# Attention over 32 heads beside a Mish layer: head quads outside, row- and column-tiled matmuls, exponentials shared by three engines, an order from a virtual clock

## The chip, the cores and the metric

The kernel runs on one core of one Trainium2 chip. A core has five engines with a queue of instructions each: TensorE (PE; the profile lists its weight loads apart, as PEld), VectorE (DVE), ScalarE (ACT), GpSimd (POOL) and SyncE (SP, which here issues DMAs). Each queue runs in its written order; the engines wait for each other through semaphores. Matmuls write to PSUM, eight banks of 512 fp32 columns on 128 partitions. The metric is the device time of one execution in microseconds; the number compared is the median of several runs. Beside it stands one profiled execution with a row for each instruction.

## The reference

x is 2048 rows (tokens) of 640, in bf16. The result is a gated mix of attention and a dense layer, both of x:

```python
g = _sigmoid((x * gate_w).sum(-1, keepdims=True))
# A: q, k, v = x @ wqkv, 32 heads of 20
scores = jnp.einsum("bhqd,bhkd->bhqk", q, k) * 20 ** -0.5
p = _softmax(scores, axis=-1)
o = jnp.einsum("bhqk,bhkd->bhqd", p, v)
a = o.reshape(B, S, D) @ wo
# B: x (640) -> 1536 -> 640
h = jnp.einsum("bsd,df->bsf", x, w1) + b1
act = h * jnp.tanh(softplus(h))          # Mish
b = jnp.einsum("bsf,fd->bsd", act, w2)
return g * a + (1 - g) * b
```

32 heads times 2048 x 2048 scores are 134 million exponentials: 1,024 tiles of 128 x 1024.

## The kernel before, in words

Queries are cut in four chunks of 512 (`qc`, the outer loop), keys in 16 tiles of 128 (`j`), heads in 16 groups of two (`g`, the middle loop). Weights for four heads are copied into zeroed tiles so that each head's 20 rows start at a multiple of 32 partitions. `emit_group` runs one group over the 16 key tiles. At each it writes the transposed scores of two heads, keys on partitions and 512 queries in columns, into one PSUM tile `Sp` of 1,024 columns (L395), two matmuls of 20 rows on different 32-row strips of the array (`tile_position`); exponentiates it in one ScalarE instruction into `E` (L406); and multiplies by V with `E` as the weights: eight loads of 128 x 128 and eight matmuls that stream 21 columns, 20 of V and a column of ones for the softmax's sum (L412), which add up in `acc`. After 16 key tiles VectorE divides by the sums (L421, L423). `Sp` and `E` have two buffers each.

The rest is cut into units in a list with a cost each: projections of k (L143), v (L186) and q (L208); the dense layer's h = x w1 with Mish from an exponential and five VectorE instructions (L223 to L243); w2 (L261); transposes of the output (L288); wo and the mix (L304 to L329). `pump_slot` is called once for each key tile: it adds `slot_credit` (460 in the first chunk, then 340) and runs units from the list while the credit pays their cost. So the order of TensorE's queue is: scores, the eight PV matmuls, perhaps a unit, the next scores. All of x comes in by one transposing DMA at the start (L88), and again for each chunk (L439).

Of the kernel before, what the change touches and what calls it, by code (L numbers as in the profile page):

```python
# [8 lines left out]
P = 128  # L10
# [3 lines left out]
BF16 = mybir.dt.bfloat16  # L14


@with_exitstack
def kernel(
# [13 lines left out]

    _, S, D = A_x.shape
    F = B_w1.shape[1]
    H = 32
    DH = D // H
    KT = D // P
    FT = F // P
    NS = S // P
    QC = 512  # L40
    NQC = S // QC
    NU = QC // P
    NPAIR = H // 4
    NG = H // 2
    ROWB = 32
    inv_sqrt_dh = float(DH) ** -0.5
    CB = 512
    CH = CB // 2

    x2d = A_x[0]  # L50
    out2d = out[0]

    consts = ctx.enter_context(tc.tile_pool(name="consts", bufs=1))
    wqp = consts.tile([P, KT, NPAIR, P], BF16, tag="wqp")
    ident = consts.tile([P, P], BF16, tag="ident")
    wo_sb = consts.tile([P, KT, D], BF16, tag="wo_sb")
    w1_sb = consts.tile([P, KT, F], BF16, tag="w1_sb")
    w2_sb = consts.tile([P, FT, D], BF16, tag="w2_sb")
    b1bf = consts.tile([P, FT], BF16, tag="b1bf")
    b1f = consts.tile([P, FT], F32, tag="b1f")  # L60
    g_t = consts.tile([P, NS], F32, tag="g_t")
    kT_all = consts.tile([P, NPAIR, S], BF16, tag="kT_all")
    VA = consts.tile([P, NS, H, DH + 1], BF16, tag="VA")

    aps = ctx.enter_context(tc.tile_pool(name="aps", bufs=2, space=bass.MemoryType.PSUM))
    xtc_pool = ctx.enter_context(tc.tile_pool(name="xtc", bufs=2))
    qtc_pool = ctx.enter_context(tc.tile_pool(name="qtc", bufs=3))
    e_pool = ctx.enter_context(tc.tile_pool(name="e_pool", bufs=2))
    opool = ctx.enter_context(tc.tile_pool(name="opool", bufs=1))
    otpool = ctx.enter_context(tc.tile_pool(name="otpool", bufs=1))  # L70
    actpool = ctx.enter_context(tc.tile_pool(name="actpool", bufs=1))
    mishp = ctx.enter_context(tc.tile_pool(name="mishp", bufs=2))
    bpool = ctx.enter_context(tc.tile_pool(name="bpool", bufs=2))
    smallp = ctx.enter_context(tc.tile_pool(name="smallp", bufs=2))
    dpool = ctx.enter_context(tc.tile_pool(name="dpool", bufs=1))
    outp = ctx.enter_context(tc.tile_pool(name="outp", bufs=2))

    xt_ctx = ExitStack()
    xt_ctx.__enter__()
    xtpool = xt_ctx.enter_context(tc.tile_pool(name="xtpool", bufs=1))  # L80
    xT = xtpool.tile([P, KT, S], BF16, tag="xT")

    stage_ctx = ExitStack()
    stage_ctx.__enter__()
    stpool = stage_ctx.enter_context(tc.tile_pool(name="stpool", bufs=1))
    Wq = stpool.tile([P, KT, D], BF16, tag="Wq")
    nc.scalar.dma_start(Wq, A_wqkv[:, 0:D].rearrange("(kt p) c -> p kt c", p=P))
    nc.sync.dma_start_transpose(  # L88
        out=xT[:, :, :], in_=x2d.rearrange("s (kt p) -> s kt p", p=P)
    )  # L90
    wv0 = xtpool.tile([P, KT, 4 * DH], BF16, tag="wvp", bufs=2)
    nc.scalar.dma_start(
        out=wv0[:, :, :],
        in_=A_wqkv[:, 2 * D : 2 * D + 4 * DH].rearrange("(kt p) c -> p kt c", p=P),
    )
    gw = xtpool.tile([P, KT, 1], BF16, tag="gw")
    nc.scalar.dma_start(gw, gate_w.rearrange("(kt p o) -> p kt o", p=P, o=1))
    wk0 = xtpool.tile([P, KT, P], BF16, tag="wkp", bufs=2)
    nc.gpsimd.memset(wk0, 0.0)
    for r in range(4):  # L100
        col0 = 64 * (r // 2) + ROWB * (r % 2)
        nc.scalar.dma_start(
            out=wk0[:, :, col0 : col0 + DH],
            in_=A_wqkv[:, D + r * DH : D + (r + 1) * DH].rearrange(
                "(kt p) c -> p kt c", p=P
            ),
        )
    nc.sync.dma_start(b1bf, B_b1.rearrange("(ft p) -> p ft", p=P))
    nc.gpsimd.dma_start(wo_sb, A_wo.rearrange("(kt p) c -> p kt c", p=P))
    nc.gpsimd.dma_start(w1_sb, B_w1.rearrange("(kt p) c -> p kt c", p=P))  # L110
    nc.gpsimd.dma_start(w2_sb, B_w2.rearrange("(ft p) c -> p ft c", p=P))

    nc.gpsimd.memset(wqp, 0.0)
    for h in range(H):
        p, r = divmod(h, 4)
        col0 = 64 * (r // 2) + ROWB * (r % 2)
        nc.gpsimd.tensor_copy(
            out=wqp[:, :, p, col0 : col0 + DH],
            in_=Wq[:, :, h * DH : (h + 1) * DH],
        )  # L120
    stage_ctx.__exit__(None, None, None)
    make_identity(nc, ident)
    nc.vector.tensor_copy(b1f, b1bf)
    nc.gpsimd.memset(VA, 1.0)

    def kt_units(p, wk=None):
        if wk is None:
            wk = xtpool.tile([P, KT, P], BF16, tag="wkp", bufs=2)
            nc.gpsimd.memset(wk, 0.0)
            for r in range(4):  # L130
                h = 4 * p + r
                col0 = 64 * (r // 2) + ROWB * (r % 2)
                nc.sync.dma_start(
                    out=wk[:, :, col0 : col0 + DH],
                    in_=A_wqkv[:, D + h * DH : D + (h + 1) * DH].rearrange(
                        "(kt p) c -> p kt c", p=P
                    ),
                )

        def chunk(sc):  # L140
            pk = aps.tile([P, CB], F32, tag="t")
            for kt in range(KT):
                nc.tensor.matmul(  # L143
                    pk[:, 0:QC],
                    lhsT=wk[:, kt, 0:P],
                    rhs=xT[:, kt, sc * QC : (sc + 1) * QC],
                    start=(kt == 0),
                    stop=(kt == KT - 1),
                )
            nc.vector.tensor_copy(  # L150
                out=kT_all[:, p, sc * QC : (sc + 1) * QC], in_=pk[:, 0:QC]
            )

        return [(1200, (lambda sc=sc: chunk(sc))) for sc in range(NQC)]

    def v_units(p, wv=None):
        if wv is None:
            wv = xtpool.tile([P, KT, 4 * DH], BF16, tag="wvp", bufs=2)
            nc.sync.dma_start(
                out=wv[:, :, :],  # L160
                in_=A_wqkv[:, 2 * D + 4 * p * DH : 2 * D + 4 * (p + 1) * DH].rearrange(
                    "(kt p) c -> p kt c", p=P
                ),
            )

        def unit(st):
            pv = aps.tile([P, CB], F32, tag="t")
            for kt in range(KT):
                lhsT = xT[:, kt, st * P : (st + 1) * P]
                if p == 0:  # L170
                    nc.tensor.matmul(  # L171
                        pv[:, 0 : 4 * DH],
                        lhsT=lhsT,
                        rhs=wv[:, kt, :],
                        start=(kt == 0),
                        stop=False,
                    )
                    nc.tensor.matmul(
                        pv[:, 4 * DH : 4 * DH + 1],
                        lhsT=lhsT,  # L180
                        rhs=gw[:, kt, 0:1],
                        start=False,
                        stop=(kt == KT - 1),
                    )
                else:
                    nc.tensor.matmul(  # L186
                        pv[:, 0 : 4 * DH],
                        lhsT=lhsT,
                        rhs=wv[:, kt, :],
                        start=(kt == 0),  # L190
                        stop=(kt == KT - 1),
                    )
            nc.vector.tensor_copy(  # L193
                out=VA[:, st, 4 * p : 4 * p + 4, 0:DH],
                in_=pv[:, 0 : 4 * DH].rearrange("p (h d) -> p h d", d=DH),
            )
            if p == 0:
                nc.scalar.activation(
                    g_t[:, st : st + 1], pv[:, 4 * DH : 4 * DH + 1], ACT.Sigmoid
                )  # L200

        return [(260, (lambda st=st: unit(st))) for st in range(NS)]

    def qt_unit(p, xTc, qTc_p):
        def unit():
            pq = aps.tile([P, CB], F32, tag="t")
            for kt in range(KT):
                nc.tensor.matmul(  # L208
                    pq[:, 0:QC],
                    lhsT=wqp[:, kt, p, 0:P],  # L210
                    rhs=xTc[:, kt, 0:QC],
                    start=(kt == 0),
                    stop=(kt == KT - 1),
                )
# [131 lines left out]
    def drain_qt(key):  # L346
        fn = qt_pending.pop(key, None)
        if fn is not None:
            fn()
# [177 lines left out]
```

## Time and profile before

| | |
|---|---|
| runs | 1363.54, 1373.24, 1375.19 us; median 1373.24 |
| the profiled execution, first to last instruction | 1383.0 us, 28,359 instructions |
| TensorE busy | 1235.3 us (89%), 12,384 matmuls |
| TensorE weight loads | 589.6 us (43%), 12,384 |
| ScalarE busy | 1053.3 us (76%) |
| VectorE busy | 463.9 us (34%) |
| GpSimd busy | 28.6 us (2%) |
| granted TensorE clock, mean | 0.608 |
| first matmul, first exponential, end of the last exponential | 44.4, 64.3, 1367.6 us |

A line of the costliest groups reads: line of the kernel, engine, operation, output<-inputs, shapes, count | busy us, mean ns of one | idle time of the engine just before, and what ended most of it. The busy time of an engine is the time in which at least one of its instructions runs; matmuls overlap, so a busy TensorE need not be streaming at its peak. The clock is the share of full speed that TensorE was granted.

### The profile page before, as it was taken

Reading aid. Unit: us, or ns where it says so; the run is one execution under the profiler, and the core shown is the slowest. Engines: PE = TensorE matmul, PEld = TensorE weight load, DVE = VectorE, ACT = ScalarE, POOL = GpSimd, SP = SyncE. Lnnn points to the kernel's source line nnn. Section 1 sums busy time; section 2 is a strip of 40 time slices with the busy share of each in tenths; the row PEclk is TensorE's granted clock in tenths of the full one; section 3 lists DMA queues with packets and bytes.
Section 4 is the critical chain, followed back from the end, with each engine's and each line's share of the span. In section 5 each row is a group of like instructions: output and inputs, shape, how many; then the busy total and the mean of one; then the engine's idle time right before and its main releaser. Section 6 shows DMA issues by size and latency. Waiting matters only on the chain.

```text
span 1383.0 us, 28359 instructions
## 1 busy us (share of the span) xinstructions
PE 1235.3 (89%) x12384; PEld 589.6 (43%) x12384; DVE 463.9 (34%) x1093; ACT 1053.3 (76%) x1138; POOL 28.6 (2%) x51
## 2 busy tenths in 40 slices
PE   0699999988999988998889998998889988998887
PEld 0354444544444444443434444443434444453333
DVE  0222222377722576410101477410001476510002
ACT  0286666987768877698998777698998787699995
POOL 7000000000000000000000000000000000000000
PEclk9975555975585555795555555695555555695555
DMA  9600000000000000000000000000000000000000
GB/s 185 109 8 7 8 7 7 2 1 1 13 8 11 11 1 1 1 21 1 1 1 11 11 1 1 1 2 1 1 2 6 16 2 1 1 2 1 1 1 20
DMA packets 53086, 16.91 MB, mean 12 GB/s; under 512 B 49408, under 2 KB 52096, under 8 KB 52960
## 3 DMA queue, kind: packets, MB, share of 16 engines
q1 hardware_dynamic: 47456, 9.30, 4.6%
q0 software_dynamic: 912, 4.75, 1.2%
q10 hardware_dynamic: 4592, 1.03, 0.6%
q8 instruction: 97, 1.59, 0.5%
q14 instruction: 29, 0.24, 0.1%
HBM read 7.21 MB, written 2.62 MB: 7 GB/s over the span
## 4 chain that ended last, share of the span: by engine, by line
PE 67%; ACT 25%; issue 3%; DMA 3%; DVE 1%; ACTq 0%
PE Sp L395 26%; ACT E L406 25%; PE acc L412 15%; PE ph L223 8%; PE pk L143 5%; PE pb L261 4%; DMA xT<-in_A_x_dram 3%; PE pq L208 3%; PE pa L304 3%; PE pv L186 3%; PE pt L288 1%; ACTq L406 0%; PE pv L171 0%; ACT e_sb L231 0%; DVE d L311 0%
## 5 line engine op out<-in xcount | busy, mean ns | idle before, releaser
L406 ACT ACTIVATE E<-Sp 128x1024 bf16<-128x1024 f32 x1024 | 1006.0, 1022 | 223.6 <-PE Sp L395 213.0
L395 PE MATMUL Sp<-qTc_p,kT_all 20*128 20x512 bf16 x2048 | 589.2, 559 | 0.0
L412 PEld LDWEIGHTS <-E 128*128 128x128 bf16 x8192 | 335.7, 106 | 471.1 <-ACT E L406 376.9
L412 PE MATMUL acc<-VA,E 128*128 128x21 bf16 x8192 | 398.1, 182 | 95.5 <-ACT E L406 93.5
L241 DVE RECIPROCAL rd<-rd 128x256 f32<-128x256 f32 x96 | 167.4, 1744 | 0.8
L395 PEld LDWEIGHTS <-kT_all 20*128 20x128 bf16 x2048 | 104.3, 98 | 51.5 <-issue 18.2
L223 PE MATMUL ph<-xTc,w_sb 128*128 128x256 bf16 x480 | 119.0, 403 | 0.1
L421 DVE RECIPROCAL rden<-acc 128x8 f32<-128x8 f32 x64 | 12.4, 193 | 297.4 <-PE acc L412 297.4
L223 PEld LDWEIGHTS <-w_sb 128*128 128x128 bf16 x480 | 51.7, 128 | 57.4 <-issue 42.6
L234 DVE SCALAR_TENSOR_TENSOR e_sb<-e_sb 128x256 f32<-128x256 f32 x96 | 40.4, 421 | 100.5 <-ACT e_sb L231 99.6
L215 DVE CAST qTc_p<-pq 128x512 bf16<-128x512 f32 x32 | 22.1, 691 | 148.8 <-PE Sp L395 98.6
L231 ACT ACTIVATE e_sb<-ph,b1f 128x256 f32<-128x256 f32 x96 | 45.4, 473 | 33.8 <-PE ph L223 29.9
L143 PE MATMUL pk<-xT,wk 128*128 128x512 bf16 x140 | 66.0, 548 | 0.0
L208 PE MATMUL pq<-xTc,wqp 128*128 128x512 bf16 x160 | 64.5, 492 | 0.0
L261 PE MATMUL pb<-w_sb,actT 128*128 128x512 bf16 x192 | 58.0, 419 | 0.1
L150 DVE CAST kT_all<-pk 128x512 bf16<-128x512 f32 x32 | 22.1, 691 | 96.3 <-PE pk L143 96.3
L186 PE MATMUL pv<-wv,xT 128*128 128x80 bf16 x560 | 50.7, 237 | 0.0
L193 DVE CAST VA<-pv 128x80 bf16<-128x80 f32 x128 | 30.4, 243 | 57.7 <-PE pv L186 51.5
L143 PE MATMUL pk<-xT,wk_118 128*128 128x512 bf16 x20 | 7.2, 544 | 44.4 <-DMA xT<-in_A_x_dram 44.4
L243 DVE SCALAR_TENSOR_TENSOR actT<-ph,b1f,rd 128x256 bf16<-128x256 f32 x96 | 45.8, 478 | 0.1
L186 PEld LDWEIGHTS <-xT 128*128 128x128 bf16 x560 | 33.4, 117 | 23.2 <-issue 23.0
L261 PEld LDWEIGHTS <-actT 128*128 128x128 bf16 x384 | 28.5, 101 | 33.3 <-issue 24.1
(101 smaller groups left out, 351.9 us busy)
## 6 DMA issues: line engine op xcount, KB each, us to landing
w_sb<-in_B_w_dram POOLq DMA_DIRECT2D x2, 1920.0 KB, 31.1
out_dram<-ot SPq DMA_DIRECT2D x16, 160.0 KB, 1.8
Wq<-in_A_wqkv_dram ACTq DMA_DIRECT2D x1, 800.0 KB, 4.9
wo_sb<-in_A_wo_dram POOLq DMA_DIRECT2D x1, 800.0 KB, 24.5
wv<-in_A_wqkv_dram SPq DMA_DIRECT2D x7, 100.0 KB, 2.3
wk<-in_A_wqkv_dram SPq DMA_DIRECT2D x28, 25.0 KB, 2.6
wv_114<-in_A_wqkv_dram ACTq DMA_DIRECT2D x1, 100.0 KB, 10.7
wk_118<-in_A_wqkv_dram ACTq DMA_DIRECT2D x4, 25.0 KB, 29.7
```

The costliest lines, as they stand in the source:

```text
L143: nc.tensor.matmul(pk[:, 0:QC], lhsT=wk[:, kt, 0:P], rhs=xT[:, kt, sc * QC : (sc + 1) * QC], start=(kt == 0), stop=(kt == KT - 1),)
L186: nc.tensor.matmul(pv[:, 0 : 4 * DH], lhsT=lhsT, rhs=wv[:, kt, :], start=(kt == 0), stop=(kt == KT - 1),)
L208: nc.tensor.matmul(pq[:, 0:QC], lhsT=wqp[:, kt, p, 0:P], rhs=xTc[:, kt, 0:QC], start=(kt == 0), stop=(kt == KT - 1),)
L223: nc.tensor.matmul(ph[:, 0:CH], lhsT=w1_sb[:, kt, ft * P : (ft + 1) * P], rhs=xTc[:, kt, half * CH : (half + 1) * CH], start=(kt == 0), st ...
L231: nc.scalar.activation(e_sb, ph[:, 0:CH], ACT.Exp, bias=b1f[:, ft : ft + 1], scale=1.0)
L241: nc.vector.reciprocal(out=rd, in_=rd)
L243: nc.vector.scalar_tensor_tensor(out=actT[:, ft, half * CH : (half + 1) * CH], in0=ph[:, 0:CH], scalar=b1f[:, ft : ft + 1], in1=rd, op0=AL ...
L261: nc.tensor.matmul(tile_[:, 0 : col1 - col0], lhsT=actT[:, ft, u * P : (u + 1) * P], rhs=w2_sb[:, ft, col0:col1], start=(ft == 0), stop=(f ...
L304: nc.tensor.matmul(pa[:, :], lhsT=oT[:, ct, u * P : (u + 1) * P], rhs=wo_sb[:, ct, 0:CB], start=(ct == 0), stop=(ct == KT - 1),)
L395: nc.tensor.matmul(Sp[:, QC * t : QC * (t + 1)], lhsT=kT_all[base + ROWB * t : base + ROWB * t + DH, p, j * P : (j + 1) * P,], rhs=qTc_p[b ...
L406: nc.scalar.activation(E[:, :], Sp[:, :], ACT.Exp, scale=inv_sqrt_dh)
L412: nc.tensor.matmul(acc[:, u, t, 0 : DH + 1], lhsT=E[:, QC * t + P * u : QC * t + P * (u + 1)], rhs=VA[:, j, h, 0 : DH + 1], start=first, s ...
```

## The change

The kernel is written anew; the launch is the same. What it does:

- **Loops.** The outer loop is now over quads of four heads, the inner one over the four query chunks (`GROUPS`: for the first six quads all chunks of a quad in a row; quads 6 and 7 chunk by chunk). A group is one quad and one chunk: 16 key tiles x 2 head pairs = 32 units of 128 x 1024 scores. There are 32 groups, 1,024 units. The output of quads 0 to 5 is parked in DRAM (`on_d`) and read back for wo, which runs over quads with zero-padded weights (`wop`).
- **Scores** (`emit_score`, `try_score`): two matmuls of 32 rows (20 and zeros) for a unit; two units together, four row strips, if two score slots are free. Three slots of two PSUM banks, two in the opening.
- **PV** (`emit_pv`): E is the moving operand, 512 columns, and V (20 columns and one of ones, 32 wide) the weights, on a 32-column strip for each head. The four heads of a quad add up in one PSUM bank on four partition strips.
- **Exponentials.** 746 units by ScalarE. The other 278 as bit lines: a VectorE multiply and add turns scores into 16-bit integers that, read as bf16, are a piecewise linear curve near the exponential (`psum_chord`); two copies of that, shifted by 35 and 83, are made by GpSimd, or the first by VectorE (`chord`), and PV adds all three. This approximates the exponential; `CH_OFF` sets the level of the lines so that their sum equals the exponential on average. ScalarE's units are exponentials as before.
- **Normalizing** (`acc_out`): a group's sums go by DMA to 128 partitions, are inverted, go through DRAM and back broadcast over partitions, and GpSimd multiplies.
- **The rest.** x is loaded in 16 plain tiles and transposed by TensorE. Mish is one ScalarE function on 128 x 3072, eight calls. The gate is two exponentials and reciprocals. (1-g) b is parked in DRAM (`b_d`).
- **Order.** `Plan` is a virtual clock with an assumed duration for every instruction. `poll_pe`, `poll_act`, `poll_dve`, `poll_gp` and `poll_sp` choose an engine's next instruction when the clock says the engine is free; the order that comes out is written into the queues. `Misc` units (projections and so on) have due times in score units and take one PSUM bank (three in the opening).

The diff, cut to its core:

```diff
+GROUPS = [(p, c) for p in range(6) for c in range(NQC)]
+for _c in range(NQC):
+    GROUPS += [(6, _c), (7, _c)]
...
+    LAT = {"PE": 130.0, "ACT": 110.0, "DVE": 90.0, "GP": 120.0, "SP": 0.0}
...
+    def run(self, eng, occ, done=None, lat=None):
+        self.free[eng] = self.t + occ
+        end = self.t + (occ if lat is None else lat) + self.LAT[eng]
...
+    def emit_score(n, slot):
+        g, p, c, kt, pair = uinfo(n)
+        for t in range(2):
+            r = 2 * pair + t
+            mm(
+                ps[:, 2 * slot + t, :],
+                kT[32 * r : 32 * r + 32, p % 3, kt * P : (kt + 1) * P],
+                qT[32 * r : 32 * r + 32, (4 * p + c) % 8, :],
+                True,
+                True,
+                (32 * r, 0),
+            )
+
+    def pe_run(mode, dur, done=None):
+        if pe_mode[0] != mode:
+            dur += 60.0
+            pe_mode[0] = mode
+        pl.run("PE", dur, done)
...
+        if n % 2 == 0 and len(ring_free) >= 2:
+            a, b = ring_free.pop(0), ring_free.pop(0)
+            emit_score(n, a)
+            emit_score(n + 1, b)
+            pe_run("R", 235.0, lambda: scored([(n, a), (n + 1, b)]))
+            return True
...
+        for t in range(2):
+            for pair, e in items:
+                n, ap, rel, last = e
+                _, p, c, kt, _ = uinfo(n)
+                h = 4 * p + 2 * pair + t
+                r = 2 * pair + t
+                mm(
+                    ps[32 * r : 32 * r + 32, ACCB, :],
+                    VA[:, kt, h * VS : h * VS + 32],
+                    ap[:, t * QC : (t + 1) * QC],
+                    ...
+                    (0, 32 * r),
+                )
...
+        pe_run("C", 235.0, done)
...
+    def poll_pe():
+        if try_score():
+            return True
+        if started and try_misc(-(10**9)):
+            return True
+        if len(eafree) <= 2 or len(ecfree) < 3:
+            if try_pv():
+                return True
+        if try_misc(40):
+            return True
+        if try_pv():
+            return True
+        if try_misc(400):
+            return True
...
+            nc.scalar.activation(a, a, ACT.Mish)
...
+            nc.scalar.activation(EA[:, e, :], ps[:, 2 * slot : 2 * slot + 2, :].rearrange("p b n -> p (b n)"), ACT.Exp, scale=SCALE)
...
+            pl.run("ACT", 950.0, done, lat=1040.0)
...
+    def chord(eng, e0, e, k):
+        if eng is nc.gpsimd and gpform(e0, k):
+            eng.tensor_tensor(
+                out=EC[:, e, :].bitcast(I32), in0=EC[:, e0, :].bitcast(I32), in1=(c35 if k == 1 else c83), op=ALU.add
+            )
+        else:
+            eng.tensor_scalar(out=EC[:, e, :], in0=EC[:, e0, :], scalar1=float(CH_ADD[k]), scalar2=1.0, op0=ALU.add, op1=ALU.mult)
...
+    def psum_chord(slot, e, k):
+        nc.vector.tensor_scalar(
+            out=EC[:, e, :],
+            in0=ps[:, 2 * slot : 2 * slot + 2, :].rearrange("p b n -> p (b n)"),
+            scalar1=CH_MUL,
+            scalar2=CH_OFF + CH_ADD[k],
+            op0=ALU.mult,
+            op1=ALU.add,
+        )
...
+    GPD = 1150.0
...
+        if not filled or len(ecfree) < 3 or open_state["lent"]:
+            return False
+        if len(filled) < 2 and pl.free["ACT"] - pl.t < 500.0:
+            return False
+        if gp_backlog() > 3500.0:
+            return False
+        n, slot = filled.pop(0)
...
+        two = gp_backlog() > 1700.0
...
+        def f1():
+            for r in range(4):
+                nc.sync.dma_start(out=den[32 * r : 32 * r + 32, b, :], in_=accs[32 * r + DH : 32 * r + DH + 1, b, :])
+
+        def f3():
+            nc.sync.dma_start(out=rd_d[g].rearrange("r (j i) -> (r j) i", i=16), in_=rden[:, b, :])
```

The program that this writes has 13,458 rows in TensorE's queue (6,728 matmuls and their loads) where the one before has 24,770.

## The prediction, made before the changed kernel ran

> **What bounds the kernel now.** I read the chain that ended last first, then the groups, the waits, and busy time and granted clock by stage.
>
> ```profile
> PE 67%; ACT 25%; issue 3%; DMA 3%; DVE 1%; ACTq 0%
> ...
> L406 ACT ACTIVATE E<-Sp 128x1024 bf16<-128x1024 f32 x1024 | 1006.0, 1022 | 223.6 <-PE Sp L395 213.0
> L395 PE MATMUL Sp<-qTc_p,kT_all 20*128 20x512 bf16 x2048 | 589.2, 559 | 0.0
> ...
> L412 PE MATMUL acc<-VA,E 128*128 128x21 bf16 x8192 | 398.1, 182 | 95.5 <-ACT E L406 93.5
> ```
>
> TensorE is two thirds of the chain, the exponentials a quarter. The 1,024 exponentials of 1.02 us fill 1,006 of 1,383 us, and before them ScalarE stood idle 213 us for scores: neither engine alone explains the time, they wait for each other. Next, busy time by window (window, length, PE, PEld, DVE, ACT, POOL, clock, DMA share, GB/s):
>
> ```profile
> 100.00:200.00 100.00, 100.00 (x932) 46.73 (x928) 23.91 (x82) 62.43 (x62) 1.89 (x3) 0.50 0.08 7
> ...
> 568.90:572.30 3.40, 3.40 (x9) 1.18 (x8) 0.00 (x0) 0.49 (x1) 0.00 (x0) 0.50 0.00 0
> 572.30:613.20 40.90, 40.42 (x481) 21.11 (x479) 7.51 (x23) 34.51 (x37) 0.00 (x0) 1.00 0.03 7
> 613.20:616.70 3.50, 2.97 (x42) 1.53 (x41) 0.00 (x0) 3.50 (x4) 0.00 (x0) 0.99 0.60 132
> 616.70:640.00 23.30, 20.77 (x217) 8.78 (x216) 2.13 (x11) 21.24 (x23) 0.00 (x0) 0.50 0.00 1
> ```
>
> From 100 to 200 us TensorE is busy all the time at half clock. It rose to 1.00 only after 3.4 us of nothing but 128-row, 512-column matmuls (568.9 to 572.3), and fell after 3.5 us that held only scores of 20 rows and PV. So I counted the trace's matmul rows in stretches of 3.4 us, as columns times active rows over 128. At half clock a share of 0.73 or more of what that clock can do was followed by a rise (one 0.75 was not), nothing below was; at full clock 0.36 or less was followed by a fall, 0.38 and more was not. **The clock follows how much of the array is filled**, and a score pair fills 40 of 128 rows. The mean is 0.608.
>
> Last, how matmuls follow each other at full clock (start, length, engine):
>
> ```profile
> 919.03 5.76 ACT L406 ACTIVATE E<-Sp 128x1024 bf16<-128x1024 f32 x6
> 919.69 0.61 PE L208 MATMUL pq<-xTc,wqp 128*128 128x512 bf16 x2
> ...
> 920.42 0.39 PE L395 MATMUL Sp<-qTc_p,kT_all 20*128 20x512 bf16 x2
> ...
> 920.74 0.39 PE L208 MATMUL pq<-xTc,wqp 128*128 128x512 bf16 x1
> ```
>
> Two row tiles take the 0.39 us of one, so they run together. Of the 0.32 us to the next start, 512 columns at full clock are 0.213 (two pq in 0.61 against one in 0.39 agree) and 0.107 is the **switch** of the array's tiling; over the trace it is 0.095 to 0.11 us at either clock. Six exponentials in a row take 0.96 each; starts are 0.92 apart.
>
> **The change, part by part.** Counts are from the changed program's order.
>
> *ScalarE.* 746 exponentials instead of 1,024; VectorE and GpSimd make the other 278. 746 x 0.92 = 686 us back to back. Eight Mish calls of 3,072 elements replace 96 exponentials of 0.47: at the slope between those two lengths, (1.022 - 0.473)/768 = 0.715 ns an element, 2.5 each, 20; five table loads of 1.28 (a row of before), 6. Sum 712, against 1,053.
>
> *TensorE.* Scores: 2,048 matmuls in 760 runs, most still pairs, some fours: 790 passes of 512 columns. PV now streams E against 32-column strips of V: 3,160 matmuls in 486 runs, four column strips at a time, 808 passes (a bit-line unit needs three). It was 8,192 weight loads of 128 columns with 21 streamed. Full-array work: 553,040 columns (k, q, v, h, w2, wo, transposes of x). 1,736 runs, so as many switches. At full clock: 790 x 0.213 = 169, 808 x 0.213 = 172, 553,040/2.4 GHz = 230, 1,736 x 0.10 = 174: **745 us**. At half clock the first three double: **1,316**. By the order: groups 1 to 22 of 32 take 540 or 958, groups 23 to 31, which hold little full-array work, 167 or 291.
>
> *VectorE.* 369 bit lines from PSUM. 128 columns take 0.291 and 512 take 0.691, so 1,024 about 1.22: 450. Casts, h, w2, wo at 0.24 to 0.69: 165. Sum 615 (was 464), and the Mish chain with its 167 us of reciprocals is gone. Below ScalarE, so hidden; uncovered if a 2.4 us pair of lines holds up the one bank that projections use.
>
> *GpSimd.* 465 bit lines, which no row shows. Nearest: its memset of 10,752 in 9.05 us (0.84 ns an element, 0.86 us for 1,024) and its copy of 100 elements in 264 ns (2.7 us if all of that scaled). I take 1.1, the memset's slope with the copy's fixed part, as the 264 ns is mostly start-up. 465 x 1.1 + 32 products + memsets = 570, hidden. It decides from about 1.7 us on. A PV that waits for a late line holds the scores queued behind it on TensorE, and those hold ScalarE.
>
> *DMA.* The transposing load that TensorE waited 44.4 us for goes; x comes in tiles of 160 KB (1.8 us for such a store). Each of 32 groups sends its sums through DRAM: about four transfers of 1.8 to 2.6 us, 10 us in a group of 25, on SP's queue in front of weight strips that are due two groups later. Hidden, but bare after the last group.
>
> *Clock.* Scores and PV fill (2,048 + 3,160) x 512 / 4 columns, 278 us at full clock if a column strip counts as a quarter. With 230 of full work that is 0.57 of 890 us. Groups without other work have 9 us of it in 23.3 exponentials x 0.92 = 21.4 us, 0.42: just above the fall. At half clock with TensorE saturated the share is 0.78 in groups 1 to 22 and 0.73 in 23 to 31, at or above the rise. So I expect full clock mostly, dips late. If column strips don't count, the share is 0.38, on the edge.
>
> The Trainium skill ("TensorE: Matmul & The Clock Gate", Part 1) says that about 3.4 us of sustained activity gives full clock and ties it to how busy TensorE is. The 100 us at 100% and 0.50 above contradict that wording; by the rule TensorE needs 745 us, by before's mean clock 571/0.608 + 174 = 1,113. The same page's Part 3 speaks against the change: three column tiles measured 2.38 times, not 3, which would make PV an estimated 172/0.79 = 217, 45 more; no run here shows column tiles.
>
> For column strips the trace gives two ends: together like the row pair (172), or one after another (3,160 x 0.213 = 673, 501 more). I take the first, nearest to the pair.
>
> **Sum.** Opening: first x tiles, transposes and projections about 15 us (before: first exponential at 64.3); group 0, between 27 and 48 on TensorE, 35: 50. Groups 1 to 22: TensorE 540 leads ScalarE's 22 x 21.4 + 26 = 497. I add 12%: 7% as TensorE waits for exponentials now (95 of 1,383), 5% for dips of the clock: 605. Groups 23 to 31: ScalarE 9 x 21.4 = 193, TensorE 167 to 291: 215. Tail: the last sums' round trip, wo, the store: 20 (before, 15.4 after the last exponential). 50 + 605 + 215 + 20 = 890 against the profiled 1,383.0. The median of the runs is 1,373.24, 0.993 of that: **885**.
>
> **Rivals.**
> - *All four engines mesh* (0.12): TensorE's 745 with 35 at the ends and 5%: 815. For it: 40.42 busy of 40.9 us in the full-clock window above. Against: the order is fixed by assumed durations (0.06 us a switch where rows show 0.10: 70 us too little).
> - *Half the time at half clock* (0.15): 50 + 749 + 229 + 20, the middle of the two sums: 1,050. For it: the 0.42 share, and strips that may not count.
> - *GpSimd's lines are the bound* (0.06): at 2.0 us 465 x 2.0 + 60 + 30: 1,020. At 2.7, 1,345.
> - *Column strips run in series, or the fours don't form* (0.03): 745 + 501 + 35 + 5%: 1,345.
> - *The clock never rises* (0.07, the slower side): every R and C pass and every projection at half speed: 35 + 1,316 x 1.07 = 1,443, timed 1,433. It is 35 + 1.07 x (571/c + 174), which passes 1,383 where the mean clock c falls below 0.53; before has 0.608 with worse-filled matmuls. Against it: the 0.78 share above.
>
> **Chances.** The forecast holds 0.57, 835 to 960. Range 815 to 1,020: it takes in the meshing case, the low half of the clock case and 2.0 us lines; left out are strips in series, a clock that never rises, the rest. 1% is about what a measurement can tell from no change. Faster 0.92, same 0.01, slower 0.07.
>
> **What would show it.** Clock line mostly 9s in groups 1 to 22 with fives late; four PV rows sharing a start and 0.21 to 0.22 us to the next four; exponentials under 750 of about 770 us busy; GpSimd lines near 1.1 us; first exponential near 16 us. Wrong if GpSimd's lines last over 1.7, PV rows start 0.2 apart within a four, switches to column strips cost far more than 0.1, or the wait of TensorE for EC tiles is large.

## The result and the profile after

| | before | after |
|---|---|---|
| median of the runs beside each other | 1374.22 us (1363.54 to 1389.46, 4 runs) | 968.36 us (965.14 to 976.89, 4 runs) |
| ratio to before, 95% interval | | 0.7071 [0.7021, 0.712] |
| profiled execution, first to last instruction | 1383.0 us | 968.8 us |
| granted TensorE clock, mean | 0.608 | 0.904 |

The change takes 29% off the time. The forecast was 885, with a range of 815 to 1,020: direction and range held, and the measured time lies 83 us above the forecast. The time of the kernel before moves between runs and chips (1,333 us at a granted clock of 0.65, 1,435 at 0.57), so every experiment below is compared by its ratio to the runs of before that stand beside it. Ratios compare only runs within 1.5% of the fastest of their kernel: for e3, e5, e8 and e9 that leaves three of nine runs of before (1,333 to 1,347 us, where the median of all nine is 1,386), and e4 and e11, of which one run is left, have no ratio.

From the page of the changed kernel: span, busy time of each engine, the clock line of 40 slices, and the shares of the chain that ended last.

```profile
span 968.8 us, 17309 instructions
...
PE 875.5 (90%) x6668; PEld 279.1 (29%) x6728; DVE 597.2 (62%) x695; ACT 743.2 (77%) x763; POOL 590.3 (61%) x510
...
PEclk9679999999999899997999999977975655999996
...
PE 23%; ACT 3%; DMA 2%; DVE 2%; SPq 1%; issue 1%; POOL 1%; POOLq 0%; DVEq 0%; ACTq 0%
```

TensorE is still the busiest engine and the largest share of the chain, now at 0.9 of full clock. The clock line has fives and sixes in a stretch after two thirds of the span, and sixes in the opening and at the end. (The shares of this chain add to a third only, so I don't read more from them.) The groups of the same page (line, engine, operation, output<-inputs, count | busy us, mean ns of one | idle before and what ended it):

```profile
L809 ACT ACTIVATE EA<-ps 128x1024 bf16<-128x1024 f32 x746 | 713.7, 1029 | 185.3 <-PE ps L277 179.9
L836 DVE TENSOR_SCALAR EC<-ps 128x1024 uint16<-128x1024 f32 x369 | 441.6, 1218 | 131.9 <-PE ps L277 90.4
L277 PE MATMUL ps<-qT,kT 32*128 32x512 bf16 x2048 | 349.6, 415 | 40.3 <-DVE EC L836 20.3
L823 POOL TENSOR_TENSOR EC<-EC,c 128x512 int32<-128x512 int32 x232 | 294.5, 1269 | 149.0 <-DVE EC L836 135.0
L827 POOL TENSOR_SCALAR EC<-EC 128x1024 uint16<-128x1024 uint16 x233 | 243.4, 1045 | 163.4 <-DVE EC L836 137.2
L277 PE MATMUL ps<-EC,VA 128*32 128x512 bf16 x1668 | 252.3, 416 | 6.3 <-POOL EC L823 5.6
```

No engine but TensorE is full: the exponentials waited 179.9 us for scores, and GpSimd's lines stood idle 272 us for VectorE's (135.0 and 137.2). PV waited only 5.6 us for GpSimd's lines.

A matmul's duration in these rows overlaps its neighbours, so I split TensorE's time by the starts of the matmul rows. What 512 columns take at full clock (0.213 us; for the 21-column PV matmuls of before their spacing, 0.026) is put down to their kind; what a stretch took above that at half clock is a column of its own; each switch of the tiling is 0.10; the rest is waiting.

| us | scores | PV | full array | half clock | switches | waits | before the first matmul | span |
|---|---|---|---|---|---|---|---|---|
| before | 227 | 213 | 220 | 309 | 204 | 162 | 44 | 1383.0 |
| after (60 matmul rows are missing) | 184 | 185 | 218 | 73 | 173 | 130 | 3 | 968.8 |
| after, a second profile with all rows (e10) | 184 | 185 | 230 | 62 | 173 | 118 | 3 | 958.9 |

Of the 414 us between the first two rows, **236 are half clock that is gone**. The columns streamed for scores and PV give 71, the long load at the start 41, waits 32 and switches 31. This is an account of TensorE's time, not of what each part would bring alone: where another engine sets the pace, as ScalarE does in parts of e1 below, half clock only takes the place of waits.

The windows of the changed kernel, cut at the first scores of groups 0, 1, 12 and 23 and near the last exponential (window, length, PE, PEld, DVE, ACT, POOL busy, clock, DMA share, GB/s):

```profile
16.60:63.80 47.20, 40.67 (x294) 15.64 (x299) 19.49 (x59) 27.27 (x30) 7.90 (x7) 0.71 0.45 119
63.80:380.00 316.20, 292.88 (x2337) 97.98 (x2364) 214.69 (x242) 253.02 (x258) 208.08 (x180) 0.98 0.10 22
380.00:701.90 321.90, 296.77 (x2260) 91.63 (x2283) 207.82 (x229) 255.94 (x261) 201.71 (x173) 0.94 0.13 28
701.90:938.00 236.10, 221.37 (x1640) 61.47 (x1644) 145.69 (x150) 200.58 (x209) 155.30 (x135) 0.80 0.13 37
938.00:968.80 30.80, 16.29 (x114) 8.36 (x106) 6.35 (x12) 3.77 (x5) 4.91 (x5) 0.76 0.15 44
```

Groups 1 to 22 run near full clock; groups 23 and on, which hold little full-array work, fall to 0.80.

### The profile page after: what moved, and what is told of

Read it like the earlier page. It is cut to its first block, busy times and chain, and to the rows that moved or that the text cites. A ratio compares the mean times of both kernels' runs of the same rounds, so it can differ in the third digit from the quotient of the medians.

```text
span 968.8 us, 17309 instructions
## 1 busy us (share of the span) xinstructions
PE 875.5 (90%) x6668; PEld 279.1 (29%) x6728; DVE 597.2 (62%) x695; ACT 743.2 (77%) x763; POOL 590.3 (61%) x510
## 5 line engine op out<-in xcount | busy, mean ns | idle before, releaser
L809 ACT ACTIVATE EA<-ps 128x1024 bf16<-128x1024 f32 x746 | 713.7, 1029 | 185.3 <-PE ps L277 179.9
L836 DVE TENSOR_SCALAR EC<-ps 128x1024 uint16<-128x1024 f32 x369 | 441.6, 1218 | 131.9 <-PE ps L277 90.4
L277 PE MATMUL ps<-qT,kT 32*128 32x512 bf16 x2048 | 349.6, 415 | 40.3 <-DVE EC L836 20.3
L823 POOL TENSOR_TENSOR EC<-EC,c 128x512 int32<-128x512 int32 x232 | 294.5, 1269 | 149.0 <-DVE EC L836 135.0
L827 POOL TENSOR_SCALAR EC<-EC 128x1024 uint16<-128x1024 uint16 x233 | 243.4, 1045 | 163.4 <-DVE EC L836 137.2
L277 PE MATMUL ps<-EC,VA 128*32 128x512 bf16 x1668 | 252.3, 416 | 6.3 <-POOL EC L823 5.6
L277 PE MATMUL ps<-EA,VA 128*32 128x512 bf16 x1492 | 226.5, 418 | 1.0 <-DVE accs L855 0.4
L277 PEld LDWEIGHTS <-kT 32*128 32x128 bf16 x2048 | 87.0, 92 | 314.8 <-issue 304.5
L277 PEld LDWEIGHTS <-VA 128*32 128x32 bf16 x3160 | 71.2, 96 | 160.3 <-issue 140.8
L277 PE MATMUL ps<-R,act 128*128 128x320 bf16 x384 | 75.3, 313 | 2.1 <-DVE VA L346 2.0
L277 PEld LDWEIGHTS <-R 128*128 128x128 bf16 x496 | 40.3, 101 | 74.8 <-issue 46.5
L953 POOL TENSOR_TENSOR ons<-accs,rb 128x512 bf16<-128x512 f32 x24 | 30.5, 1270 | 35.2 <-DMA rb<-rd_d 34.3
```

Source lines behind the costliest of these rows:

```text
L277: nc.tensor.matmul(outap, lhsT=l, rhs=r, start=first, stop=last, tile_position=pos, skip_group_check=True)
L809: nc.scalar.activation(EA[:, e, :], ps[:, 2 * slot : 2 * slot + 2, :].rearrange("p b n -> p (b n)"), ACT.Exp, scale=SCALE)
L823: eng.tensor_tensor(out=EC[:, e, :].bitcast(I32), in0=EC[:, e0, :].bitcast(I32), in1=(c35 if k == 1 else c83), op=ALU.add)
L827: eng.tensor_scalar(out=EC[:, e, :], in0=EC[:, e0, :], scalar1=float(CH_ADD[k]), scalar2=1.0, op0=ALU.add, op1=ALU.mult)
L836: nc.vector.tensor_scalar(out=EC[:, e, :], in0=ps[:, 2 * slot : 2 * slot + 2, :].rearrange("p b n -> p (b n)"), scalar1=CH_MUL, scalar2=CH ...
L953: gp_q.append((1300.0, lambda: nc.gpsimd.tensor_tensor(out=dst, in0=accs[:, b, :], in1=rb[:, b, :], op=ALU.mult), lambda: pl.give(("on", p ...
```

## The experiments

All edits are to the changed kernel unless the label says "before". The first question: is TensorE the bound, and how much of its time is clock, passes, switches and waits? The runs e1, e2, e6 and e4 ran on one chip, e3, e5, e8 and e9 on another, e10 to e13 on a third. The split of each run's profiled execution, as above (e3, e5, e8 and e9 lack some 60 matmul rows each, as the first profile of after does, which makes "full array" too low and "waits" too high by 10 to 15 us):

| us | scores | PV | full array | half clock | switches | waits | span |
|---|---|---|---|---|---|---|---|
| e1, no lines | 215 | 109 | 230 | 296 | 177 | 155 | 1189.4 |
| e2, fours only | 146 | 210 | 230 | 77 | 131 | 189 | 990.5 |
| e3, truer durations | 188 | 184 | 217 | 45 | 173 | 129 | 942.3 |
| e4, filling late | 184 | 183 | 245 | 47 | 176 | 117 | 958.0 |
| e5, fewer lines | 195 | 162 | 217 | 105 | 187 | 119 | 991.1 |
| e6, later due times | 183 | 184 | 230 | 24 | 173 | 106 | 906.5 |
| e8, before, fewer exponentials | 254 | 213 | 205 | 314 | 164 | 227 | 1426.2 |
| e9, before, strips | 233 | 224 | 208 | 379 | 259 | 150 | 1502.9 |
| e11, no lines, filled | 214 | 109 | 294 | 296 | 195 | 146 | 1262.0 |
| e12, e6 with e3 and another opening | 188 | 184 | 230 | 38 | 174 | 102 | 923.9 |
| e13, e12 with softer fours | 178 | 186 | 230 | 36 | 163 | 106 | 906.4 |

### e1: all exponentials on ScalarE

```diff
+        if True:
+            return False
         if len(filled) < 2 and pl.free["ACT"] - pl.t < 500.0:
```

The edit stands where `poll_dve` decides on a bit-line unit.

> The changed kernel with all 1,024 exponentials on ScalarE, no bit lines. If TensorE sets the pace of the changed kernel (my theory), it is relieved by 1,112 PV matmuls, 278 passes or 59 us, but ScalarE now needs 1,024 x 0.92 + 26 = 968 us and becomes the bound: with 17 us before the first exponential, 28 after the last and a few waits, 1,020 to 1,060. Rival: ScalarE's 185 idle us in the changed kernel show that the lines weren't needed, and the relief of TensorE counts: 930 to 970.

Measured: 1184.37 us (1171.75 to 1191.19), 0.8427 of before [0.8354, 0.85]. Both expectations missed, by more than 120 us. Its clock line, and its windows cut at the first scores of group 12 (502.8 us), near where the full-array work runs out:

```profile
PEclk9578699999556899985555555555555555565766
```
```profile
66.30:502.80 436.50, 416.77 (x2333) 126.32 (x2332) 98.35 (x164) 372.79 (x364) 13.96 (x11) 0.86 0.09 19
502.80:1163.20 660.40, 618.25 (x2911) 132.44 (x2911) 50.20 (x91) 601.60 (x641) 29.68 (x21) 0.54 0.10 25
```

From there the mean clock is 0.54 for 660 us, with short rises only, while TensorE is busy 94% of the time. Against e10 TensorE has 45 us less to stream (PV 76 less, score passes 31 more) and 234 us more of half clock. Without lines most groups of the second half have scores and PV of one E per unit and about 1 us of full-array work; saturated at half clock that is a share of 0.61 by the prediction's counting, under the 0.73 from which the clock rose in before. That fits a fallen clock that hardly comes back in these groups.

But the 234 us of half clock are not the price of it, for ScalarE has 278 more exponentials. Its group in e1's page, and then the window of group 13, with 1 us of full-array work, and that of group 20, with 5:

```profile
L809 ACT ACTIVATE EA<-ps 128x1024 bf16<-128x1024 f32 x1024 | 978.5, 1125 | 144.0 <-PE ps L277 133.3
...
534.40:564.90 30.50, 28.54 (x136) 5.51 (x135) 1.64 (x3) 29.78 (x33) 1.27 (x1) 0.50 0.05 14
756.20:795.40 39.20, 38.16 (x156) 6.99 (x155) 4.25 (x7) 30.81 (x33) 1.27 (x1) 0.50 0.04 12
```

In group 13 ScalarE is busy 29.8 of 30.5 us: it sets the pace, and the half clock costs next to nothing. In group 20 it is busy 30.8 of 39.2 us and waits for scores. Over the kernel the exponentials wait 133 us for scores, so I estimate that at most about 130 of the 230 us between the two spans are the clock's, and the rest is ScalarE's added work: without these waits e1 would be at some 1,056, the upper end of the theory. The loops, the tiling and the opening by themselves are worth 0.84, and the lines take that to 0.69 to 0.71.

### e2: scores in fours only

```diff
+        if open_state["lent"] is False and n % 2 == 0:
+            return False
         a = ring_free.pop(0)
```

> The changed kernel with scores written only when two slots are free, so always four row strips at once. If TensorE's passes and switches set the pace, the 862 score passes seen become about 520 and some 250 switches go: 73 + 25 to 50 us less, 860 to 900. Rival: the hand-over of the three slots sets the pace; two slots free at once leave ScalarE and VectorE one slot between them, ScalarE waits more, 970 to 1,050.

Measured: 997.2 us (992.39 to 997.53), 0.7112 [0.7081, 0.7144]. The rival was right: against e10, score passes fell by 38 us and switches by 42, PV rose by 25, and waits rose by 71. Four strips need both of two slots free at once; holding the pair back until then leaves ScalarE without scores:

```profile
L811 ACT ACTIVATE EA<-ps 128x1024 bf16<-128x1024 f32 x689 | 670.3, 1024 | 254.2 <-PE ps L277 251.9
```

251.9 us of waiting for scores instead of 179.9. With three slots, passes saved on TensorE are given back as waits.

### e3: truer durations in the virtual clock

```diff
-            dur += 60.0
+            dur += 100.0
-            pe_run("R", 235.0, ...)
+            pe_run("R", 215.0, ...)
-        pe_run("C", 235.0, done)
+        pe_run("C", 215.0, done)
-            pl.run("ACT", 950.0, done, lat=1040.0)
+            pl.run("ACT", 925.0, done, lat=1025.0)
```

> The changed kernel with the virtual clock's assumptions set to what the trace shows: 0.10 us for a switch of the array's tiling instead of 0.06, 0.215 for a pass of scores or PV instead of 0.235, 0.925 for an exponential instead of 0.95. If the 130 us that TensorE waits come from an order planned with wrong durations, most of the waits over 0.3 us (89 us in 91 places) shrink: 930 to 950. Rival: the waits come from three slots, one bank and queues in order, whatever the durations assumed: within 1%, 960 to 978.

Measured: 946.39 us (944.43 to 949.52), 0.7093 [0.7048, 0.7137]. The time in us is as expected, and the ratio is that of the changed kernel; but the ratio goes by the three shortest runs of before, and by the median of all nine it would be 0.683. So whether the kernel gained is not settled. The waits, which were to fall, stayed (129 against 130); half clock was 45, against 73 and 62. So the wrong durations weren't what made TensorE wait.

### e4: full-array work added where the clock was low

Fourteen units of five 128-row, 512-column matmuls, whose results nobody reads, due in groups 23 and on.

```diff
+    for i in range(14):
+        ...
+        misc.append(Misc(f"fill{i}", due_g(23.0 + 0.5 * i), [("sdone", 22)], pieces, None, 0.0, [], eng="NONE"))
```

> The changed kernel with 14 units of five 128 x 512 matmuls added in groups 23 to 30, whose result nobody reads: 15 us of TensorE work and up to 28 switches, 3 us. If the half clock from 700 to 800 us costs what its passes say (28 us there, 36 from 702 to 938), the filled array keeps the clock up and the kernel gets faster by 10 to 20 us in spite of the work: 948 to 960. Rival: the low clock there is a sign of TensorE waiting, not a cost: 975 to 990.

Measured: 962.67 us (942.81 to 966.43); over the whole kernel not to be told from the changed one. The stage itself shows more. The window of groups 23 to the last exponential in e4, and then in e10 (the changed kernel again):

```profile
705.30:928.60 223.30, 210.26 (x1729) 63.68 (x1732) 149.70 (x152) 199.67 (x210) 158.55 (x138) 0.95 0.14 38
```
```profile
690.00:934.00 244.00, 229.53 (x1681) 63.66 (x1681) 147.09 (x151) 204.66 (x212) 159.04 (x138) 0.80 0.13 37
```

With 14 x 5 x 0.213 = 15 us **more** work the stage is 21 us **shorter** (17 shorter than in the first profile of after, whose last exponential ends at 941.8), and its clock is 0.95 instead of 0.80. How busy TensorE is doesn't explain that: it was 94% busy in both. How much of the array is filled fits it. The order alone moves this clock too, though by less: without filling it was 0.82 in e2 and 0.89 in e3.

### e5: fewer lines

```diff
-        if gp_backlog() > 3500.0:
+        if gp_backlog() > 3500.0 or stat["dve"] >= 0.18 * nxt[0]:
```

839 exponentials on ScalarE instead of 746.

> The changed kernel with bit lines for at most 18% of the units instead of 27%: about 184 instead of 278. TensorE saves 94 x 4 PV matmuls, 94 passes, 20 us, and some switches; ScalarE gets 94 x 0.92 = 86 us more and has 180 idle. If TensorE is the bound: 940 to 960. Rival: ScalarE's idle time can't be used, because it waits for scores in places set by the slots, so its added work comes on top: 1,000 to 1,050.

Measured: 987.44 us (985.56 to 992.85), 0.7399 [0.7343, 0.7455]. Between the two expectations, and in us 2 to 3% longer than the changed kernel, on another chip. Against e10 the passes of scores and PV and the switches are 2 us more in sum, waits 119 against 118, and half clock 105 against 62: fewer lines cost clock, as in e1.

### e6: full-array work spread to later groups

```diff
-                add_h(c, f, due_g(11.0 + 4.5 * (k - 24) / 24))
+                add_h(c, f, due_g(13.0 + 6.0 * (k - 24) / 24))
-                add_w2(t, half, due_g(16.5 + 5.0 * (k - 16) / 16))
+                add_w2(t, half, due_g(21.5 + 4.5 * (k - 16) / 16))
```

The expectation names w2 only; the edit also moved the due times of h, as the diff shows. The order takes such units early and w2 waits for Mish of h, so I think the line for h does most of it; the two weren't run apart. By the traces, groups 12 to 18 hold 7 to 12 us of full-array columns each in e10 and 5 to 7.5 in e6; groups 23 to 25 hold at most 1.3 in e10 and 5 to 6.4 in e6.

> The changed kernel with the second half of the w2 matmuls (192 of 320 columns, 26 us at full clock) due in groups 21 to 26 instead of 16 to 21. If TensorE is the bound in groups 1 to 22 and short of work and clock in groups 23 to 26, about 26 us leave the first stage and the clock of the second stays up (36 us were lost to half clock there): 925 to 945. Rival: the waits between engines set the pace everywhere: within 1% of the changed kernel, 960 to 978.

Measured: 908.41 us (907.85 to 914.52), 0.6499 [0.646, 0.6539]: 17 us shorter than the lower end of the theory. The clock line of e6, and its windows of groups 1 to 22 and 23 to the last exponential:

```profile
PEclk9779999999999999999999999999999978999996
```
```profile
61.30:658.20 596.90, 563.72 (x4551) 182.06 (x4547) 404.44 (x449) 509.22 (x520) 413.38 (x359) 1.00 0.11 24
658.20:877.60 219.40, 205.31 (x1758) 65.33 (x1755) 154.14 (x162) 199.78 (x211) 163.18 (x139) 0.95 0.17 46
```

The same work in another order: half clock 24 us instead of 62 to 73, waits 106 instead of 118 to 130, everything else within 2 us of e10. This beats both kernels; the prediction's 605 for groups 1 to 22 is 597 here, and its 215 for the late groups is 219.

### e8 and e9: single parts of the change, made to the kernel before

e8 takes every fourth exponential off ScalarE, without the lines; PV reads a fixed tile there instead.

```diff
+            if j % 4 == 3:
+                E = E0
+            else:
```

> The kernel before with every fourth exponential left out (a fixed tile of ones stands in for E at every fourth key tile; scores and PV matmuls stay): what taking a quarter of the exponentials off ScalarE is worth by itself, without TensorE's part of the change. My theory, TensorE at half clock is the main bound of the kernel before: only the 26 of 64 groups paced by ScalarE at 1.05 us a tile gain, about 0.15 us a tile, and some waits of TensorE go: 1,270 to 1,330. Rival: ScalarE's exponentials set the pace, 256 x 1.02 = 261 us go: 1,110 to 1,150.

Measured: 1423.29 us (1411.37 to 1434.6), 1.0625 [1.0471, 1.078]. No faster than before, with a quarter of ScalarE's main work gone. How much slower it is can't be told: the runs of before beside it reach from 1,333 to 1,435. This page's busy line and the exponentials' group:

```profile
PE 1232.5 (86%) x12315; PEld 557.9 (39%) x12384; DVE 460.8 (32%) x1093; ACT 805.9 (57%) x882; POOL 29.6 (2%) x52
...
L411 ACT ACTIVATE E<-Sp 128x1024 bf16<-128x1024 f32 x768 | 757.6, 1022 | 488.2 <-PE Sp L397 481.7
```

ScalarE is 247 us less busy and waits 269 more for scores. The scheduler also put TensorE's queue in another order (three score matmuls in a row in places), and TensorE's waits rose from 162 to 227 (10 to 15 of that may be missing rows). So relief of ScalarE alone brings nothing here, but the run doesn't say what it would bring with the old order.

e9 streams E against 32-column strips of V in the kernel before, two strips at a time (shown in part). The softmax's division has the same instructions here, on 21 partitions and on elements that are not the right ones.

```diff
-                for u in range(NU):
-                    nc.tensor.matmul(acc[:, u, t, 0 : DH + 1], lhsT=E[...], rhs=VA[:, j, h, 0 : DH + 1], ...)
+                nc.tensor.matmul(
+                    acc[32 * t : 32 * t + DH + 1, 0:QC],
+                    lhsT=VA[:, j, h, 0 : DH + 1],
+                    rhs=E[:, QC * t : QC * (t + 1)],
+                    tile_position=(0, 32 * t), ...
+                )
```

> The kernel before with PV as in the changed kernel: E streams, 512 columns for each of the two heads, on two 32-column strips of V (the softmax's division works on the wrong elements here, with the same instructions on 21 partitions, so that part of the computation is changed). 8,192 weight loads and as many matmuls of 21 columns go, 2,048 matmuls of 512 columns come. If what counts is how many strips run together, two are too few: a key tile takes TensorE 0.427 + 0.427 + two switches of 0.1 at half clock, 1.05 us instead of 0.85, and the clock stays at half (share 0.33): 1,420 to 1,520. Rival: the 336 us of weight loads are the cost, and moving E alone is the gain: 1,200 to 1,300.

Measured: 1504.76 us (1503.43 to 1504.97), 1.1263 [1.1226, 1.1299], within the theory's range; against the longest run of before beside it, 1,435, it is 5% longer. By twos a PV pass saves nothing against the eight short matmuls it replaces (224 against 213), switches rise by 55 us and half clock by 70. In the changed kernel, with the quads in the loop, the strips run by fours and PV takes 185.

### e10: the changed kernel once more

> The changed kernel once more, unchanged, as the yardstick for the three beside it on the same chip: 960 to 980 by either theory.

Measured: 961.35 us (956.84 to 964.4), 0.6941 [0.6894, 0.6988]. Its profile has all matmul rows: 860 score and 868 PV passes, 1,731 switches. The two measurements of the same kernel, 0.7071 and 0.6941, lie further apart than their intervals: ratios from different chips that differ by less than 2% are not read as different here.

### e11: no lines, with filling

e1 with 60 filling units as in e4, three a group from group 12.

```diff
+    for i in range(60):
+        ...
+        misc.append(Misc(f"fill{i}", due_g(12.0 + 0.33 * i), [("sdone", int(12.0 + 0.33 * i) - 1)], pieces, None, 0.0, [], eng="NONE"))
```

> The kernel without bit lines (1,184 us, clock 0.67) with 60 units of five 128 x 512 matmuls added, three for each group from 12 on, whose result nobody reads: 64 us of TensorE work at full clock and up to 120 switches. Without lines, groups 13 to 31 took 33 us each at half clock, where ScalarE needs 32 x 0.92 = 29.4. If it is the clock that was lost with the lines' PV matmuls, the filled array brings it back and these groups go to 29.5 to 30.5 us: 1,110 to 1,150. Rival: TensorE was simply full there, and the added work comes on top: 1,220 to 1,260.

Measured: 1236.55 us (1190.44 to 1263.76, the shorter the higher the clock, 0.76 to 0.70). The window of the second part in the profiled execution, the longest of the four:

```profile
506.10:1236.40 730.30, 689.04 (x3211) 153.69 (x3211) 50.28 (x91) 610.91 (x641) 29.69 (x21) 0.61 0.09 23
```

The forecast missed: the clock went from 0.54 only to 0.61, and here the work came on top. The shortest run is about as long as e1 in spite of 64 us more of work, so with these four the two aren't told apart. Counted as before, the share when saturated at half clock is 0.67 with this filling, still under 0.73. That fits the rule, but was worked out afterwards; no run here had enough filling to bring e1's clock back.

### e12 and e13: edits put together

e12 is e6 with e3's durations and all tiles of x copied by VectorE in the opening. e13 is e12 and a softer form of e2: hold back a pair only while ScalarE still has a filled slot.

```diff
+        if n % 2 == 0 and filled and open_state["lent"] is False:
+            return False
```

> The changed kernel with three edits: h and w2 of the second half due later (908 us by itself), the virtual clock's durations as measured (22 us less by itself), and x tiles 1 and 3 copied by VectorE instead of ScalarE, whose queue stands behind weight loads for 8.9 us at the start (4.8 us of wait). If waits by wrong durations and the clock lost for want of work are separate costs: 875 to 895. Rival: both gains were the same lost clock: 900 to 915.

> The same three edits, and single score pairs only when no written slot waits for an exponential, so that fours form where nobody starves: by the order 288 runs of four and 385 of two instead of 202 and 530, 100 switches fewer. If TensorE's passes and switches still set the pace: 20 + 10 us less than with the three edits, 850 to 875. Rival: the slots' hand-over sets it, as with fours only (PV waited 73 us more there): as long as with the three edits or up to 20 us longer.

Measured: e12 931.9 us (925.68 to 937.24), 0.6729 [0.6673, 0.6785]; e13 903.19 us (896.87 to 908.17), 0.6508 [0.6453, 0.6563]. e12 met neither expectation. On the same chip it is 3% shorter than e10, but by the ratios it is slower than e6 alone, so nothing of what e3 seemed to gain shows on top of e6; half clock is 38 against 24 and scores 188 against 183, but the chip was another one too, so why is not settled. The step from e12 to e13, on one chip, is in the direction of the theory: passes and switches fall by 19 us and waits rise by 4 only, where e2's waits had eaten all of it. Its level, 903, is above what was expected, since e12 was. Both e6 and e13 beat the changed kernel; they can't be told apart (0.6499 and 0.6508, on different chips; e13 is 6% shorter than e10 on its own).

## Why the prediction was right, and by what it was off

**What held.** *Strips by fours.* From the timeline of the changed kernel near 302 us (start, length, engine, line):

```profile
302.30 0.39 PE L277 MATMUL ps<-EC,VA 128*32 128x512 bf16 x1
302.30 0.39 PE L277 MATMUL ps<-EA,VA 128*32 128x512 bf16 x1
302.30 0.39 PE L277 MATMUL ps<-EC,VA 128*32 128x512 bf16 x1
302.31 0.39 PE L277 MATMUL ps<-EA,VA 128*32 128x512 bf16 x1
...
302.63 0.39 PE L277 MATMUL ps<-qT,kT 32*128 32x512 bf16 x2
...
302.95 0.40 PE L277 MATMUL ps<-EC,VA 128*32 128x512 bf16 x4
303.17 0.38 PE L277 MATMUL ps<-EA,VA 128*32 128x512 bf16 x1
```

Four start together, to 0.01 us; the next kind starts 0.33 and 0.32 later (0.213 and a switch of 0.10 to 0.11), the next four of the same kind 0.22 later. Taking strips as together, by the nearest row of before, was right. The Trainium skill ("TensorE: Matmul & The Clock Gate", Part 3) gives 2.38 for three column tiles; these rows show four for the time of one, so the estimate of 217 us for PV that the prediction made from that page doesn't hold here.

*Engines.* 746 exponentials; ScalarE 743.2 us busy (forecast 712; an exponential took 0.957 us of busy time and not 0.92, as they seldom follow back to back); VectorE 597.2 (615; a bit line 1,218 ns, 1.22 forecast); GpSimd 590.3 (570; its lines 1,045 and 1,269 ns, 1.1 forecast). The uncertain price of GpSimd's lines, 0.86 to 2.7, was taken well, and PV waited 5.6 us for them: that rival is out. The first exponential started at 17.0 us (16 forecast).

*The clock by the array's fill.* Nines through groups 1 to 22, fives late, as forecast. In the trace of after, counting a column strip as a quarter, each fall followed a stretch of 3.4 us at full clock with a share of 0.36 or less (two such stretches were followed by none). Rises are less sharp: most followed 0.68 and more at half clock, two came after 0.57 and 0.61, and several stretches of 0.70 to 0.76 were followed by none. The prediction's bounds were 0.36 and 0.73. The experiments for it are e4, with more work in less time, e6, with the same work in less, and e5, with fewer passes and more half clock. The Trainium skill ("TensorE: Matmul & The Clock Gate", Part 1), which the prediction set against the rows, ties the clock to being busy; e1's 660 us at 94% and 0.54 contradict that again.

**What was off: 83 us, by stage.** (79 of them lie between the sum of 890 and the profiled execution; the rest is between that execution and the median.)

| stage | forecast | after | difference |
|---|---|---|---|
| opening and group 0 | 50 | 63.8 | 14 |
| groups 1 to 22 | 605 | 638 | 33 |
| groups 23 to 31 | 215 | 236 | 21 |
| tail | 20 | 31 | 11 |

- **"I add 12%"** for groups 1 to 22 is the term that failed most. By the split of after, passes and switches there take 541 us (forecast 540; somewhat more with the missing rows), half clock 20 (5%, 27, forecast) and waits **77, where 7%, or 38, was forecast**. The 7% was taken from TensorE's wait for exponentials in the kernel before, 95 us, where the split above counts 162 us of waits in all. How I read the difference: with three slots the engines hold each other up in turn, as ScalarE waited 179.9 us for scores and the scores 40.3 us, half of that for a bit line that still held a slot. e6 shows that a part of it goes with another placing of the full-array work (waits of 106 over the kernel, not 118 to 130). How much more slots would give wasn't tried.
- **Groups 23 to 31**, "TensorE 167 to 291", "215": 131 us of passes, 43 of switches, 36 of half clock and 26 of waits. The dips forecast here came: 36 us, 29% of the 124 that lie between the two ends. But 215 left 48 us for dips and waits together where they took 62, and passes and switches took 174 and not 167. With the passes that ran, the saturated share at half clock is 0.69 here by the prediction's counting, and not the 0.73 that it had. To the last exponential at 941.8, e4 took 17 us off by filling and e6 20 by moving work there.
- **790 and 808 passes** were really 860 and 868 (e10). That is 130 x 0.213 = 28 us over the kernel. For PV most of it was in the order to be seen: counted by strips, where a pair of strips that follows itself makes two passes, the order holds 849. For scores it holds 790, but in 66 of its 202 runs of four matmuls the second pair started more than 0.02 us after the first, released by a bit line (50 times) or an exponential (16) that had still held its slot.
- **The opening**: group 0 was to take 35 us; it took 47.2 at a clock of 0.71. The forecast's 27 to 48 held both ends; the clock decided it.
- **The tail**, "20": from the timeline of the changed kernel:

```profile
947.33 0.69 DVE L855 COPY accs<-ps 128x512 f32<-128x512 f32 x1 [7.14 <-PE ps L277]
948.05 2.41 SPq L934 DMA_DIRECT2D den<-accs  x4
951.72 0.25 DVE L944 RECIPROCAL rden<-den 128x16 f32<-128x16 f32 x1 [3.70 <-DMA den<-accs]
...
957.14 1.26 POOL L953 TENSOR_TENSOR R<-accs,rb 128x512 bf16<-128x512 f32 x1 [14.41 <-DMA rb<-rd_d]
958.46 7.00 PE L277 MATMUL ps<-R,R 128*128 128x320 bf16 x29 [11.17 <-POOL R L953]
```

The last exponential ends at 941.8, and PV goes on for 5.5 us. Then the round trip of the sums keeps TensorE idle for 11.2 us, and 7.0 us of wo and a store follow. The forecast had the round trip and the store, but neither the PV behind the last exponential nor all of wo.

The rivals: "half the time at half clock" (1,050) and "the clock never rises" (1,433) are out for this order. The low clock that they assume is real, as e1 and, in part, e5 show: the lines' extra PV passes help to keep it away. "All four engines mesh" (815) was not reached by any run; e13's 903 is nearest. "Strips in series" is out by the timeline.

## What to carry to other kernels

On this chip count how much of the array each stretch of TensorE's queue fills before you count its work: taking passes off a tiled kernel can cost clock (e5, e1), and spreading the full-array work evenly among row and column strips was worth 5 to 8% for two changed lines (e6). Before you put lost time down to the clock, look whether another engine is full there: in most groups of e1's second half ScalarE was. Strips paid when all four ran together; by twos, with a switch of 0.1 us between kinds, they lost 5 to 13% (e9). A gain in passes that needs two free buffers at once must be paid in buffers, or it returns as waits (e2; softened, e13).

## What the runs showed of the hardware that I had not expected

- A fallen clock can stay down. In e1 660 us ran at 0.54 with TensorE 94% busy, and 64 us of filling matmuls spread over them raised that to 0.61 only in the profiled execution (e11). What it costs depends on the group: next to nothing where ScalarE was full.
- More work in less time: 15 us of matmuls added, 17 to 21 us less in their stage (e4).
- A switch between row strips, column strips and the full array costs about the same in every direction seen, 0.095 to 0.115 us, at either clock (from the full array to row strips at half clock often 0.14, in e1).
- GpSimd's additions on integers, 1.27 us for 128 x 512 in int32 and 1.05 for 128 x 1024 in uint16, were neither the bound nor late, with 590 us of work beside VectorE's 597.
